# Two products of wo in split precision: M from hi and lo pieces in three one-pass matmuls a group

## The chip, the cores and the metric

The kernel runs on 1 core of a Trainium2 chip. The metric is device time in microseconds (us) for one execution, the median of several. TensorE (PE) does the matmuls, VectorE (DVE), ScalarE (ACT) and GpSimd (POOL) the element-wise work, and SyncE (SP) issues all DMA transfers. Each engine runs its own instructions in the order in which they were written, and waits on semaphores of the others.

## The reference

Two layers; each is a linear-attention block and an MLP with residuals, on 2048 rows of 448 floats (16 heads of 28, MLP width 1792).

```python
def _A_ref(x, wqkv, wo):
    qkv = (lambda x, *d: x.transpose(*d))((x @ wqkv).reshape(B, S, 3, H, Dh), 2, 0, 3, 1, 4)
    q, k, v = qkv[0], qkv[1], qkv[2]
    phi = lambda t: jnp.where(t > 0, t + 1, jnp.exp(t)) + 1e-6
    pq, pk = phi(q), phi(k)
    kv = jnp.einsum("bhsd,bhse->bhde", pk, v)
    z = jnp.einsum("bhsd->bhd", pk)
    num = jnp.einsum("bhqd,bhde->bhqe", pq, kv)
    den = jnp.einsum("bhqd,bhd->bhq", pq, z)[..., None] + 1e-6
    o = num / den
    return (lambda x, *d: x.transpose(*d))(o, 0, 2, 1, 3).reshape(B, S, D) @ wo
...
x = x + _A_ref(_layernorm(x, axis=-1), A_wqkv, A_wo)
x = x + _B_ref(_layernorm(x, axis=-1), B_w1, B_b1, B_w2, B_b2)
x = x + _A_ref(_layernorm(x, axis=-1), A_wqkv, A_wo)
x = x + _B_ref(_layernorm(x, axis=-1), B_w1, B_b1, B_w2, B_b2)
```

## The kernel before, in words

Float32 matmuls take several passes on TensorE. Nearly all products are therefore split: an operand x becomes hi (rounded to the one-pass type, by a copy on ACT) and lo = x - hi (on DVE or POOL), and hi*hi + hi*lo + lo*hi is summed in PSUM by three one-pass matmuls. Few products are left in plain float32, among them the one this case is about.

A layer has three parts.

**Phase 1** walks over 16 tiles of 128 rows (`phase1`, steps t = 0 to 15). Each step has a list of tokens (`STEP`, `STEPS`) that is carried out in that order: K projects a tile to k (`stage_k`), `kp`, `kh`, `kl` make phi(k) and its hi and lo (ek on ACT, L323 and L324; psk on DVE, L326; kh on ACT, L446; kl on DVE, L455) and add it to the running sum `za` (L462), `s` splits the normalized x (xnh on ACT, L428; xnl on POOL, L429), G adds x^T phi(k) of the tile before to four PSUM banks (`stage_g`, L508 to L512), Q projects to q (`stage_q`, psq), and in layer 0 `bg` splits a piece of an MLP weight behind that (hi w2h on ACT, L365; lo w2l on POOL, L366). In the last step the sum za becomes zh (ACT, L465) and zl (DVE, L468). After step 11 the piece of wqkv for v is loaded, and after step 13 `trans_load` issues two DMAs for `wo` (the tile wot, L643): groups 0 and 1 in the first, groups 2 and 3 in the second.

**The transition** (token list `ORDER`) turns these sums into one matrix M for the layer, 448 x 448 in four groups of 112 rows (four heads each). `z` multiplies zh and zl with ones (zp, L649) and makes zb (ACT, L651) and dc (DVE, L654, L655). `gt` copies G out of PSUM, `kv` multiplies it with wv into kvp (L669), `mask` keeps the blocks on the diagonal (kvm, L673). `m0` to `m3` each multiply a group of kvm with a group of wo (L679, PSUM mp), and `ms0` to `ms3` split the result into Mh (ACT, L691) and Ml (DVE, L692). Meanwhile the first four tiles of phi(q) are loaded, multiplied with zb (`qz`, pz on POOL, L722), divided by their denominators (`qs`: dn, L728 and L729, rd, L731, and pq, L733, all on DVE), transposed on PE (`tq`, L740) and split (`qq`: qh on ACT, L749, ql on DVE, L750); `Qp` gives phi(q) of a late tile (three ACT instructions, L496 to L498, and an addition on POOL, L499). `o0` to `o3` multiply with M (L760 to L762), and `la`, `lb` add the residual and normalize.

**The MLP** runs over four blocks of 512 rows (L829 to L849), with the attention output of the next block made behind it.

Buffers come from tagged pools: "H" has nine of 448 floats (tiles of x), "xn" and "F" two each of 512, "S" five of 1024. A new tile waits until the last user of an old one in its tag is done. In the last steps of layer 0 the "xn" buffers hold pieces of w2; "F" holds kl, zl and later the last Ml.

The order of the transition, cut to the part around M:

```python
    ORDER = (
        "Q ld1 z ld0 ld2 qz0 qz1 G gt qs1 Q Qp kv qs0 tq1 Q mask qz2 tq0 qs2 ld3 b "
        "m0 qq1 Qp m1 qz3 Qp ms0 qq0 m2 ms1 m3 ms2 tq2 ms3 qs3 o0 la0 qq2 o1 tq3 lb0 tu0 la1 qq3 "
```

Of the kernel before, what the change touches and what calls it, by code (L numbers as in the profile page):

```python
# [12 lines left out]
OP = mybir.AluOpType  # L13
# [9 lines left out]
def linear_attn_mlp_kernel(  # L23
# [43 lines left out]
    def t448(tag, bufs, name, dt=F32):  # L67
        bufs = NH if tag == "H" else bufs
        return work.tile([128, D], dt, name=name, tag=tag, bufs=bufs)
# [4 lines left out]
    def f(ap):  # L74
        return ap.bitcast(F32)
# [426 lines left out]
    def stage_g(l, t, acc):  # L502
# [16 lines left out]


    ORDER = (
# [3 lines left out]
    )  # L525
# [54 lines left out]
    def phase1(l, tr):  # L580
        za = consts.tile([128, D], F32, name="za", tag="za")
        acc = []
        load_to(l, 4 if l == 0 else NORM[l][1][-1])
        if l == 0:
            launch(za)
            load_to(l, NORM[l][2][-1])
        for t in range(l == 0, NT):
            norm = NORM[l][t] if t < len(NORM[l]) else ()
            for tok in STEPS.get((l, t), STEP).split():
                if tok[1:].isdigit() and tok[0] in "anv":  # L590
                    {"a": stage_a, "n": stage_n, "v": stage_t}[tok[0]](l, int(tok[1:]))
                elif tok == "q1":
                    stage_qphi(1)
                elif tok == "sp":
                    for key, h in list(stored):
                        block(key)
                        spread(key, h)
                elif tok == "ld" and t + 2 < len(NORM[l]):
                    load_to(l, NORM[l][t + 2][-1])
                elif tok == "a":  # L600
                    for u in norm:
                        stage_a(l, u)
                elif tok == "n":
                    for u in norm:
                        stage_n(l, u)
                elif tok == "tu":
                    for u in norm:
                        stage_t(l, u)
                elif tok == "T" and t + 1 < NT:
                    stage_b(l, t + 1, "acc" if t == 1 else "h")  # L610
                elif tok == "X" and t + 1 < NT and (l == 0 or t + 1 >= 4):
                    stage_x(l, t + 1)
                elif tok == "K":
                    stage_k(l, t)
                elif tok == "qp":
                    stage_qphi()
                elif tok == "kp":
                    stage_kphi(l, t)
                elif tok == "kh":
                    stage_kh(l, t)  # L620
                elif tok == "kl":
                    stage_kl(l, t, za)
                elif tok == "s":
                    stage_s(l, t)
                elif tok == "G" and t >= 1:
                    acc = acc or [bank("acc", 4, f"G{c}")[:, :D] for c in range(4)]
                    stage_g(l, t - 1, acc)
                elif tok == "bg" and l == 0:
                    background(BG[t], 1 if t >= 8 else 2)
                elif tok == "Q" and t < DEFER:  # L630
                    stage_q(l, t)
            if t == 11:
                tr.wv = stage_square(wqkv[:, 2 * D:])
            if t == 13:
                trans_load(l, tr)
        return za, acc


    def trans_load(l, tr):
        tr.wo = []  # L640
        for h in range(2):
            s = half("wot")[:G, :2 * D].rearrange("p (g n) -> p g n", g=2)
            sp.dma_start(s, wo[h * 2 * G:(h + 1) * 2 * G, :].rearrange("(g p) n -> p g n", p=G))  # L643
            tr.wo += [s[:, 0], s[:, 1]]

    def trans_z(tr, za):
        zp = bank("m", 2, "zp")[:, :D]
# [16 lines left out]
    def trans_kv(tr):  # L664
        tr.kvp = bank("m", 2, "kvp")[:G, :D]
        for g in range(NG):
            s = slice(g * G, (g + 1) * G)
            for c in range(4):
                pe.matmul(tr.kvp[:, s], tr.wv[c][:, s], tr.gt[c][:, s], start=(c == 0), stop=(c == 3))  # L669

    def trans_mask(tr):
        tr.kvm = t448("W6", 1, "kvm")[:G]
        dve.tensor_tensor(tr.kvm.rearrange("p (g d) -> p g d", g=NG),  # L673
                          tr.kvp.rearrange("p (g d) -> p g d", g=NG),
                          mask[:, None, :].to_broadcast([G, NG, G]), op=OP.mult)

    def trans_m(tr, g):
        mp = bank("acc", 4, "mp")[:G, :D]
        pe.matmul(mp, tr.kvm[:, g * G:(g + 1) * G], tr.wo[g], start=True, stop=True)  # L679
        tr.mp[g] = mp  # L680

    def trans_ms(tr, g):
# [263 lines left out]
    warm_up(2)  # L946

    for l in range(LAYERS):
        tr = SimpleNamespace(mp={})
        za, acc = phase1(l, tr)  # L950
        if l == 0:
            background(0)
        fill = list(range(DEFER, NT))

        def biases(j):
            if l == 0:
                sp.dma_start(b1s, b1.rearrange("(c p) -> p c", p=128))
                sp.dma_start(b2b, b2[None, :].to_broadcast([128, D]))

        def pre(j):  # L960
            for k in range(4):
                load_pq(l, 1, k)
            if l == 0:
                background(2)

        tok_ = SimpleNamespace(
            Q=lambda j: stage_q(l, fill.pop(0)), Qp=lambda j: fill_qphi(), Qv=lambda j: stage_qphi(j or 9),
            Qa=lambda j: stage_q(l, fill.pop(0), tag="acc"), G=lambda j: stage_g(l, NT - 1, acc),
            ld=lambda j: (load_pq(l, 0, j), load_x(l, j)), z=lambda j: trans_z(tr, zs[l]), gt=lambda j: trans_gt(tr, acc),
            kv=lambda j: trans_kv(tr), mask=lambda j: trans_mask(tr), m=lambda j: trans_m(tr, j),  # L970
            ms=lambda j: trans_ms(tr, j), qz=lambda j: q_z(l, 0, j, tr), qs=lambda j: q_scale(l, 0, j, tr),
            tq=lambda j: q_transpose(l, 0, j), qq=lambda j: q_split(l, 0, j), o=lambda j: o_mm(l, 0, j, tr),
            la=lambda j: o_ln(l, 0, j), lb=lambda j: o_n(l, 0, j), T=lambda j: m_transpose(l, 0, j),
            x=lambda j: m_split(l, 0, j), tu=lambda j: turn(xns.pop(("m", l, j)), ("m", l, 0), j),
            st=lambda j: store_sq(("m", l, 0), 0), sp=lambda j: spread(("m", l, 0), 0), pre=pre, b=biases)
        for tok in ORDER.split():
            name, j = tok.rstrip("0123456789"), int("0" + tok.lstrip("abcdefghijklmnopqrstuvwxyzQTG"))
            getattr(tok_, name)(j)
        assert not fill and not qo
        table(AF.Gelu_apprx_tanh)  # L980
        q_z(l, 1, 0, tr)
        mlp1(l, 0, 0)
        trans_chunks(tr)
        for b in range(NB):
            acc = [bank("acc", 4, f"y{j}")[:, :D] for j in range(4)]
            nxt = b + 1 < NB
            if not nxt and l + 1 < LAYERS:
                st_k = stage_square(wqkv[:, D:2 * D])
                st_q = stage_square(wqkv[:, :D])
                load_to(l + 1, PRE - 1)  # L990
            for i in range(NF):
                if i + 1 < NF:
                    mlp1(l, b, i + 1)
                elif nxt:
                    mlp1(l, b + 1, 0)
                if l == 0 and b == 0 and i:
                    background(1, 1)
                if i == NF - 2 and not nxt and l + 1 < LAYERS:
                    table(AF.Exp)
                if 9 <= i < 13:  # L1000
                    add_bias(l, b, i - 9)
                if nxt:
                    behind(l, b, i, tr)
                elif l + 1 < LAYERS:
                    if i == 2:
                        split_kq("k", st_k)
                    if i == 5:
                        split_kq("q", st_q)
                    if i in (3, 4, 6, 7, 8):
                        t = (3, 4, 6, 7, 8).index(i)  # L1010
                        stage_a(l + 1, t)
                        stage_n(l + 1, t)
                        stage_t(l + 1, t)
                        if t % 2:
                            stage_sp(l + 1, t)
                    if 9 <= i < 13:
                        stage_x(l + 1, i - 9)
                mlp2(l, b, i, acc)
# [28 lines left out]
```

## Time and profile before

| | us |
|---|---|
| median of 3 runs | 877.67 (877.45 to 877.82) |
| profiled execution, its own time | 878.36 |
| profiled execution, span from first to last instruction | 876.6 |
| PE busy in the span | 871.2 (99%) |
| DVE, ACT, POOL busy | 491.0, 344.2, 221.4 |

All times inside the span are counted from its first instruction. A row of the timeline gives the start, the duration, engine, line, operation, tiles (out<-in) and shape of an instruction or of a run of equal ones, and in brackets the idle time of the engine before it and what ended it. The transition of layer 0 lies at 104 to 139 us, that of layer 1 at 534 to 569 us. Instructions of an engine overlap a little, so that the distance between starts is shorter than a duration.

### The profile page before, as it was taken

The page shows a single profiled execution, that of the slowest core. Times are in us where ns is not written, and L with a number is a line of the kernel's source. Part 1 is how long each engine was busy: PE and PEld are TensorE (multiplying, and loading weights), DVE is VectorE, ACT ScalarE, POOL GpSimd, SP SyncE. Part 2 cuts the span into 40 slices and gives each one's busy share as a digit, 9 for nine tenths or more (in the row PEclk, how much of TensorE's full clock was granted, in tenths as well). Part 3 has the DMA queues.
Part 4 walks back from the last instruction along what each step waited for, and adds up shares of the span by engine and source line. Part 5 has one row for each costly group of instructions (what it writes and reads, how often), then busy time and mean ns, then how long its engine had stood idle before and what let it go on. Part 6 is the DMA issues. An engine that isn't in the chain of part 4 may idle for free.

```text
span 876.6 us, 11680 instructions
## 1 busy us (share of the span) xinstructions
PE 871.2 (99%) x4180; PEld 772.3 (88%) x4180; DVE 491.0 (56%) x957; ACT 344.2 (39%) x604; POOL 221.4 (25%) x250
## 2 busy tenths in 40 slices
PE   9999999999999999999999999999999999999998
PEld 8999988888888888888899998888888888888887
DVE  6878595658455443226467876864674473433112
ACT  5676635324223322333355665332233133223221
POOL 5566532335012102011222344120220140140000
PEclk9999999999999999999999999999999999999999
DMA  5475636624313402051145543352332413111001
GB/s 158 138 225 164 208 88 203 191 85 133 132 59 104 156 0 97 1 179 49 48 135 184 169 133 106 101 184 81 108 111 91 135 68 116 49 49 42 1 1 43
DMA packets 63482, 94.76 MB, mean 108 GB/s; under 512 B 8896, under 2 KB 58560, under 8 KB 63424
## 3 DMA queue, kind: packets, MB, share of 16 engines
q1 hardware_dynamic: 63424, 94.01, 33.4%
q8 instruction: 33, 0.54, 0.3%
q14 instruction: 25, 0.20, 0.1%
HBM read 56.17 MB, written 34.60 MB: 104 GB/s over the span
## 4 chain that ended last, share of the span: by engine, by line
PE 98%; DMA 1%; DVE 0%; issue 0%; POOL 0%; SPq 0%; POOLq 0%; DVEq 0%
PE y L849 10%; PE y L848 10%; PE y L847 10%; PE hp L830 9%; PE hp L829 9%; PE hp L831 9%; PE hp L832 3%; PE hp L833 3%; PE psk L313 2%; PE psq L312 2%; PE G L510 2%; PE psq L314 2%; PE G L508 2%; PE G L509 2%; PE psq L313 2%; PE psk L314 2%
## 5 line engine op out<-in xcount | busy, mean ns | idle before, releaser
L839 DVE TENSOR_TENSOR gl<-g,gh 128x512 fp32r<-128x512 f32 x112 | 82.6, 737 | 299.8 <-ACT gh L838 299.8
L835 ACT ACTIVATE g<-hp,b1s 128x512 f32<-128x512 f32 x112 | 77.1, 688 | 406.3 <-PE hp L833 403.4
L849 PE MATMUL y<-w2h,gl 128*128 128x448 f32 x448 | 163.7, 365 | 0.0
L848 PE MATMUL y<-w2l,gh 128*128 128x448 f32 x448 | 163.6, 365 | 0.0
L847 PE MATMUL y<-w2h,gh 128*128 128x448 f32 x448 | 163.6, 365 | 0.0
L830 PE MATMUL hp<-XH,w1l 128*128 128x512 f32 x336 | 131.5, 392 | 0.0
L829 PE MATMUL hp<-XH,w1h 128*128 128x512 f32 x336 | 131.2, 391 | 0.0
L831 PE MATMUL hp<-XL,w1h 128*128 128x512 f32 x336 | 131.2, 391 | 0.0
L209 POOL TENSOR_TENSOR brs<-bve,mhalf 128x1 f32<-128x1 f32 x64 | 39.6, 619 | 283.7 <-DVE bve L207 280.6
L847 PEld LDWEIGHTS y<-w2h,gh 128*128 128x128 f32 x448 | 84.1, 188 | 9.0
L848 PEld LDWEIGHTS y<-w2l,gh 128*128 128x128 f32 x448 | 84.1, 188 | 8.4
L849 PEld LDWEIGHTS y<-w2h,gl 128*128 128x128 f32 x448 | 84.2, 188 | 6.6
L831 PEld LDWEIGHTS hp<-XL,w1h 128*128 128x128 f32 x336 | 63.1, 188 | 14.2 <-issue 0.6
L830 PEld LDWEIGHTS hp<-XH,w1l 128*128 128x128 f32 x336 | 63.1, 188 | 11.2
L829 PEld LDWEIGHTS hp<-XH,w1h 128*128 128x128 f32 x336 | 63.1, 188 | 10.9
L838 ACT CAST gh<-g 128x512 fp32r<-128x512 f32 x112 | 69.7, 622 | 3.6
L722 POOL TENSOR_TENSOR pz<-pq,zb 128x448 f32<-128x448 f32 x32 | 36.6, 1146 | 84.4 <-DVE dn L728 69.6
L429 POOL TENSOR_TENSOR xnl<-x,xnh 128x384 fp32r<-128x384 f32 x32 | 35.0, 1093 | 72.4 <-ACT xnh L428 40.4
L302 DVE TENSOR_TENSOR XL<-sp,XH 128x512 fp32r<-128x512 f32 x50 | 44.2, 891 | 3.6 <-ACT XH L301 3.6
L833 PE MATMUL hp<-XL,w1x 128*128 128x512 f32 x112 | 43.6, 389 | 0.0
L832 PE MATMUL hp<-XH,w1x 128*128 128x512 f32 x112 | 43.6, 389 | 0.0
L791 POOL TENSOR_TENSOR x<-x,b2b 128x448 f32<-128x448 f32 x32 | 41.9, 1330 | 0.0
(152 smaller groups left out, 1567.1 us busy)
## 6 DMA issues: line engine op xcount, KB each, us to landing
x<-in_A_x_dram SPq DMA_DIRECT2D x32, 224.0 KB, 4.0
pq_d<-eq SPq DMA_DIRECT2D x32, 224.0 KB, 2.7
pq<-pq_d SPq DMA_DIRECT2D x32, 224.0 KB, 3.2
sq_m<-sq SPq DMA_DIRECT2D x14, 512.0 KB, 2.7
sp<-sq_m SPq DMA_DIRECT2D x56, 128.0 KB, 2.8
x<-x_d SPq DMA_DIRECT2D x32, 224.0 KB, 3.5
sq_a<-sq SPq DMA_DIRECT2D x12, 512.0 KB, 2.9
sp<-sq_a SPq DMA_DIRECT2D x48, 128.0 KB, 2.9
```

The source lines that it names most:

```text
L302: eng.tensor_tensor(lo.rearrange("p (c i n) -> p c i n", c=4, n=32), x, f(h), op=OP.subtract)
L829: pe.matmul(o, w1h[:, c, s], x.moving(x.hi, c), start=(c == 0), stop=False)
L830: pe.matmul(o, w1l[:, c, s], x.moving(x.hi, c), start=False, stop=False)
L831: pe.matmul(o, w1h[:, c, s], x.moving(x.lo, c), start=False, stop=False)
L832: pe.matmul(o, w1x[:, s], x.moving(x.hi, 3), start=False, stop=False)
L833: pe.matmul(o, w1x[:, s], x.moving(x.lo, 3), start=False, stop=True)
L835: act.activation(g, hp, AF.Gelu_apprx_tanh, bias=b1s[:, i:i + 1])
L838: act.copy(gh, g)
L839: dve.tensor_sub(gl, g, f(gh))
L847: pe.matmul(acc[j], gh[:, s], w2h[:, i], start=first, stop=False)
L848: pe.matmul(acc[j], gh[:, s], w2l[:, i], start=False, stop=False)
L849: pe.matmul(acc[j], gl[:, s], w2h[:, i], start=False, stop=last)
```

## The change

M is made from split operands. wo is split into woh (ACT copies, L653 of the changed kernel) and wol (DVE subtractions, L659): woh of groups 0 and 1 at the end of step 14, woh of groups 2 and 3 and wol of group 0 at the end of step 15, and wol of groups 1 to 3 at the new token `wol` behind `z`. The five buffers woh0 to woh3 and wol0 are of tag "H", wol1 and wol2 of "xn", wol3 of "F". The masked kvm is copied to kvh on ACT as part of `mask`, and kvl = kvm - kvh is made on DVE at the new token `mlo` behind `qs2`; both lie in a new "S" buffer. Each group of M is then three one-pass matmuls instead of one float32 matmul.

```diff
@@ ORDER
-        "Q ld1 z ld0 ld2 qz0 qz1 G gt qs1 Q Qp kv qs0 tq1 Q mask qz2 tq0 qs2 ld3 b "
+        "Q ld1 z wol ld0 ld2 qz0 qz1 G gt qs1 Q Qp kv qs0 tq1 Q mask qz2 tq0 qs2 mlo ld3 b "
@@ phase1, end of step t
             if t == 13:
                 trans_load(l, tr)
+            if t >= 14:
+                wo_hi(tr, (t * 2 - 28, t * 2 - 27))
+            if t == 15:
+                wo_lo(tr, (0,))
@@
+    def wo_hi(tr, gs):
+        for g in gs:
+            hi = t448("H", 8, "woh", F32R)[:G]
+            act.copy(hi, tr.wo[g])
+            tr.woh.append(hi)
+
+    def wo_lo(tr, gs):
+        for g in gs:
+            lo = (t448("H", 8, "wol", F32R) if g == 0 else t512("F" if g == 3 else "xn", 2, "wol", F32R)[:, :D])[:G]
+            dve.tensor_tensor(lo, tr.wo[g], f(tr.woh[g]), op=OP.subtract)
+            tr.wol.append(lo)
@@ trans_mask
+        s = work.tile([128, 1024], F32R, name="kvs", tag="S", bufs=5)[:G]
+        tr.kvh, tr.kvl = s[:, :D], s[:, 512:512 + D]
+        act.copy(tr.kvh, tr.kvm)
+
+    def trans_mlo(tr):
+        dve.tensor_tensor(tr.kvl, tr.kvm, f(tr.kvh), op=OP.subtract)
@@ trans_m
-        pe.matmul(mp, tr.kvm[:, g * G:(g + 1) * G], tr.wo[g], start=True, stop=True)
+        s = slice(g * G, (g + 1) * G)
+        pe.matmul(mp, tr.kvh[:, s], tr.woh[g], start=True, stop=False)
+        pe.matmul(mp, tr.kvh[:, s], tr.wol[g], start=False, stop=False)
+        pe.matmul(mp, tr.kvl[:, s], tr.woh[g], start=False, stop=True)
```

More of the change, by code (lines that the diff above doesn't have):

```diff
@@ L948, in linear_attn_mlp_kernel @@
     for l in range(LAYERS):
-        tr = SimpleNamespace(mp={})
+        tr = SimpleNamespace(mp={}, woh=[], wol=[])
         za, acc = phase1(l, tr)
@@ L969, in linear_attn_mlp_kernel @@
             ld=lambda j: (load_pq(l, 0, j), load_x(l, j)), z=lambda j: trans_z(tr, zs[l]), gt=lambda j: trans_gt(tr, acc),
-            kv=lambda j: trans_kv(tr), mask=lambda j: trans_mask(tr), m=lambda j: trans_m(tr, j),
+            kv=lambda j: trans_kv(tr), mask=lambda j: trans_mask(tr), mlo=lambda j: trans_mlo(tr), wol=lambda j: wo_lo(tr, (1, 2, 3)), m=lambda j: trans_m(tr, j),
             ms=lambda j: trans_ms(tr, j), qz=lambda j: q_z(l, 0, j, tr), qs=lambda j: q_scale(l, 0, j, tr),
```

## The prediction

> **What bounds the kernel now.** I read the engines' busy time first, then the chain that ended last, then the timeline of the transitions engine by engine.
>
> ```profile
> PE 871.2 (99%) x4180; PEld 772.3 (88%) x4180; DVE 491.0 (56%) x957; ACT 344.2 (39%) x604; POOL 221.4 (25%) x250
> PE 98%; DMA 1%; DVE 0%; issue 0%; POOL 0%; SPq 0%; POOLq 0%; DVEq 0%
> ```
>
> PE never rests: a PE instruction saved is time saved, and any wait that reaches PE is time lost. The other engines only have slack, and the question is how much of it lies where the new work goes.
>
> **M itself.** The timeline of PE in layer 0:
>
> ```profile
> 109.47 3.31 PE L669 MATMUL kvp<-gt,stg 128*112 128x112 f32 x32
> 112.61 0.60 PE L740 MATMUL tq<-ident,pq 128*112 128x128 f32 x4
> ...
> 115.72 3.17 PE L679 MATMUL mp<-wot,kvm 112*112 112x448 f32 x8
> 118.73 0.60 PE L740 MATMUL tq<-ident,pq 128*112 128x128 f32 x4
> 119.09 0.45 PE L760 MATMUL op<-Mh,qh 112*128 112x448 f32 x1
> 119.38 0.37 PE L761 MATMUL op<-Ml,qh 112*128 112x448 f32 x1
> ...
> 121.61 0.37 PE L760 MATMUL op<-Mh,qh 112*128 112x448 f32 x1
> ```
>
> The four float32 groups take 118.73 - 115.72 = 3.01 us. A one-pass matmul of the same width takes (121.61 - 119.38) / 11 = 0.203, and the first behind transposes 0.29. Twelve take 0.29 + 11 x 0.203 = 2.52. The change removes 0.49 a layer, 0.98 in all. That is all it can gain.
>
> **The copies of wo on ACT.** In layer 0 the SP queue, what the tile wot answers on its first DMA, and ACT, in this order:
>
> ```profile
> 96.97 1.50 SPq L643 DMA_DIRECT2D wot<-in_A_wo_dram  x1
> ```
> ```profile
> DMA to landing us min/median/max: 5.5/5.5/5.5
> ```
> ```profile
> 98.59 0.56 ACT L365 CAST w2h<-stg 128x448 fp32r<-128x448 f32 x1
> 99.05 0.57 ACT L428 CAST xnh<-x 128x448 fp32r<-128x448 f32 x1
> 100.19 0.54 ACT L323 ACTIVATE ek<-psk 128x448 f32<-128x448 f32 x1 [0.56 <-PE psk L317]
> ...
> 103.89 1.03 ACT L365 CAST w2h<-stg 128x448 fp32r<-128x448 f32 x2
> 105.21 0.63 ACT L651 ACTIVATE zb<-zp,zc 128x448 f32<-128x448 f32 x1 [0.29 <-PE zp L649]
> ```
>
> Groups 0 and 1 of wo land at 96.97 + 5.5 = 102.47. In the order of the changed program their two copies stand on ACT right behind the w2h of 98.59 and ahead of xnh, with a wait for that DMA. ACT keeps its order, so xnh, ek, kh and zh of tile 15, which want to start from 99.05 on, queue behind a transfer that is 3.4 us away. A copy in a row takes 0.47 (two in 1.03 with the last one's tail). The copies start near 102.53, xnh near 103.47, ek at 103.94 instead of 100.19: 3.75 late. PE beside DVE:
>
> ```profile
> 104.24 0.37 PE L317 MATMUL psq<-wq,XL 128*128 128x448 f32 x1
> ...
> 104.70 0.47 PE L649 MATMUL zp<-zl,ones 128*128 128x448 f32 x1
> ```
> ```profile
> 104.02 0.63 DVE L468 TENSOR_TENSOR zl<-za,zh 128x448 fp32r<-128x448 f32 x1 [0.16 <-ACT zh L465]
> ```
>
> zl ends at 104.65 and PE uses it at 104.70: this path has no slack. ek, psk, kh, za, zh, zl follow each other, so zp with zl moves to 108.45. PE has behind 104.24 nothing ahead of `z` in its order. **Stall in layer 0: 3.75.** From below it is the landing less the place of the copies, 102.47 - 99.06 = 3.4.
>
> In layer 1 the same pair is covered:
>
> ```profile
> 514.24 3.45 SPq L643 DMA_DIRECT2D wot<-in_A_wo_dram  x2
> ```
> ```profile
> DMA to landing us min/median/max: 5.6/6.0/6.5
> ```
> ```profile
> 527.94 0.56 ACT L428 CAST xnh<-x 128x448 fp32r<-128x448 f32 x1
> 530.01 0.55 ACT L323 ACTIVATE ek<-psk 128x448 f32<-128x448 f32 x1 [1.52 <-PE psk L317]
> ```
>
> Both have landed by 514.24 + 3.45 + 6.5 = 524.2, and two copies (0.94) fit in the 1.52 idle ahead of ek. Cost nothing. The copies of groups 2 and 3 lie behind zh. In layer 0 they put off the second w2h, and zb by about 0.6; in layer 1 there is no w2h and zb keeps its place.
>
> **wol on DVE, against POOL.** DVE and POOL in layer 1, where a denominator meets POOL's work:
>
> ```profile
> 538.05 0.62 DVE L728 TENSOR_REDUCE dn<-pz 128x16 f32<-128x448 f32 x1 [1.11 <-POOL pz L722]
> 538.70 0.17 DVE L729 TENSOR_TENSOR dn<-dn,dc 128x16 f32<-128x16 f32 x1
> ...
> 539.20 0.63 DVE L733 SCALAR_TENSOR_TENSOR pq<-pq,rd 128x448 f32<-128x448 f32 x1
> ...
> 540.38 0.92 DVE L729 TENSOR_TENSOR dn<-dn,dc 128x16 f32<-128x16 f32 x1
> ...
> 541.63 1.22 DVE L733 SCALAR_TENSOR_TENSOR pq<-pq,rd 128x448 f32<-128x448 f32 x1
> 542.77 0.61 DVE L673 TENSOR_TENSOR kvm<-kvp,mask 112x448 f32<-112x448 f32 x1
> ```
> ```profile
> 535.75 2.26 POOL L722 TENSOR_TENSOR pz<-pq,zb 128x448 f32<-128x448 f32 x2 [5.89 <-ACT zb L651]
> 540.15 1.13 POOL L499 TENSOR_TENSOR eq<-ep,eq 128x448 f32<-128x448 f32 x1 [2.14 <-ACT eq L498]
> 541.24 1.13 POOL L722 TENSOR_TENSOR pz<-pq,zb 128x448 f32<-128x448 f32 x1
> ```
>
> A DVE instruction with two inputs from SBUF does not run while such a POOL instruction runs: L729 takes 0.17 alone and 0.92 behind L499, ending where that ends (541.30, 541.28); L733 waits the same way for pz. The wol and kvl subtractions are of this kind. They cost 0.55 each when alone, and up to one POOL instruction (1.13) more, and hold POOL up in turn.
>
> The Trainium skill ("SBUF — State Buffer", Who interferes with whom) calls this an exclusive lock that the earlier issue gets for a whole instruction; by it a subtraction that comes first would wait for nothing. The trace shows the waiting side only.
>
> *Layer 1.* wol0 fits behind zl. dc ends as before, and pz runs until 535.75 + 2.26 = 538.01. wol1 waits for it, and the three end at 538.01 + 3 x 0.55 = 539.65, where dn started at 538.05: DVE is 1.5 late. L729 then meets L499 (until 541.3), rd and pq of tile 1 end at 542.25. The next pz waits for the buffer that the second dn (until 542.8) reads, so it runs 542.85 to 544.0 and blocks pq of tile 0 until 544.55. kvm moves from 542.77 to 544.5, its copy kvh ends at 545.7, and qs2 (dn, L729, rd, L733: 1.6) and kvl follow kvm on DVE: kvl ends at 547.3.
>
> PE around M in layer 1:
>
> ```profile
> 545.55 3.17 PE L679 MATMUL mp<-wot,kvm 112*112 112x448 f32 x8
> 548.56 0.60 PE L740 MATMUL tq<-ident,pq 128*112 128x128 f32 x4
> ```
>
> The second row lies 429.83 behind its twin in layer 0 (118.73), and I carry PE's, ACT's and DVE's rows of layer 0 over by that. M started at 545.55; now it starts at 545.75, when kvh is there, and its third matmul waits for kvl until 547.35. The other nine follow at 0.203, and M ends at 549.55 instead of 548.56 (0.17 of it a weight load not hidden).
>
> Then ACT, and DVE behind it, in layer 0:
>
> ```profile
> 113.25 0.59 ACT L749 CAST qh<-tq 112x512 fp32r<-112x512 f32 x1 [3.01 <-PE tq L740]
> ...
> 116.81 0.53 ACT L691 CAST Mh<-mp 112x448 fp32r<-112x448 f32 x1
> ```
> ```profile
> 118.52 1.68 DVE L692 TENSOR_TENSOR Ml<-mp,Mh 112x448 fp32r<-112x448 f32 x3
> ```
>
> kvh stands on ACT ahead of qh, so qh and the six Qp instructions behind it (3.56 with 0.44 of idle: 3.1 of work) wait for it. qh starts at 545.6, and Mh0 at 545.6 + 3.1 = 548.7 instead of 116.81 + 429.83 = 546.64, and Ml0, ql, Ml1 to Ml3 end at 552.15 instead of 118.52 + 1.68 + 429.83 = 550.03. `o0` is fed by these one at a time and hands over to `o1` at 552.7 instead of 551.44. **Layer 1: +1.3**, the 0.49 of M included.
>
> *Layer 0*, in old times (3.75 taken off). zb is late by 0.6, the two w2l on POOL (1.13 each) come ahead of pz, and wol0, dc's second instruction and wol1 to wol3 alternate with POOL's w2l, pz, pz and L499. wol3 ends at 112.6. The row this moves, and its cover:
>
> ```profile
> 109.05 0.62 DVE L728 TENSOR_REDUCE dn<-pz 128x16 f32<-128x448 f32 x1 [2.23 <-POOL pz L722]
> ```
>
> The 2.23 idle would hold three subtractions of 0.55 if nothing else moved. With the alternation dn starts at 112.55, 3.5 late; pq of tile 1 is ready at 114.3 where `tq1` wanted it at 112.61 (stall 1.7). The rest goes as in layer 1: kvm at 116.5, kvl until 119.3, M over at 121.35 instead of 118.73, `o1` at 124.7 instead of 121.61. **Layer 0 behind the stall: +3.2**, with 0.1 for ql of tile 2.
>
> Behind `o3` DVE has idle again, and the loads of x and of wq are not issued later than PE moves. New buffers: "S" gets one more tile between wv and Mh, released long before; the "H" tiles take buffers of x tiles 7 to 11. Both cost nothing; I see no gain or loss but in the two transitions.
>
> **Sum.** 3.75 + 3.2 + 1.3 = 8.25 on the profiled execution's 878.36 (span 876.6): 886.6. That execution lies 0.69 over the median of the runs, 877.67, so the forecast is 885.9. Bounds of the lock: if wol and kvl cost 0.55 each and never wait, dn is 0.3 late in both layers and the kvh, qh, Mh order on ACT alone is left, about +0.4 and +0.1 with M's gain in: 3.75 + 0.5 = 4.25, 881.9. If kvl also waits for a POOL instruction in each layer, 2 x 1.13 more: 888.2.
>
> **Rivals.**
> - *The stall without the lock* (881.9). For: which engine gets in first is a race, and 2.23 and 1.11 of idle stand ahead of dn. Against: L729 and L733 show the blocking, and POOL has instructions waiting. 0.20.
> - *PE goes cold in its 3.3 us of idle.* At the start of the kernel PE is slow:
>
> ```profile
> 1.50 4.64 PE L162 MATMUL warm<-ones 128*128 128x128 f32 x20 [1.50 <-DVE ones L157]
> ```
>
>   0.232 each, against 3.14 / 32 = 0.098 for kvp's 112 columns, or 0.112 for 128. If PE falls back to that half rate for 4.64 us, it loses 2.3: 888.2. 0.10. The Trainium skill ("TensorE: Matmul & The Clock Gate", Part 1) has the clock halved after a window of about 3.4 us without work, from 104.6 to 107.8 here nearly one. No gap of that size stands in this trace behind the start, and the granted clock reads 1.00 even there.
> - *Faster.* The mechanism is the copies of wo finding their data there. It takes a landing before 99.06, so an issue before 93.6; SP issues wot at 96.97, behind transfers that the change does not touch. Then only the lock is left, and if that does not bite either, M's 0.98 gives 878.36 - 0.98 - 0.69 = 876.7. 0.03, of which 0.01 for the lock eating the gain.
> - *Beyond 889*, more waits than I followed: 0.05.
>
> The change does what it says: PE's order has the twelve matmuls in place of the four, so that is no rival.
>
> **How the numbers follow.** The forecast, stall and lock, has 0.62. The range 881.5 to 888.8 holds it, the stall without the lock, kvl waiting on top, and the cold PE; it leaves out some 0.1 to 0.15. Two thousandths are 1.8 us, about what can be told from no change: faster 0.02, same 0.01, slower 0.97.
>
> **What would show it.** Right: ACT idle for over 3 us ahead of L653 in layer 0, ended by the DMA of wot; PE idle about as long ahead of zp; L659 rows longer than 0.62; a PE wait ahead of the third matmul of M (L704); twelve matmuls in 2.5 plus that wait. Wrong: woh copies in layer 0 that start before 100, wol rows of 0.6 and dn within 0.5 of its place, or matmul spacing of 0.4 behind zp.

## The result, and the profile after

The changed kernel takes **884.50 us** (median of 6 runs, 884.17 to 885.74) against 877.75 (6 runs, 877.43 to 878.22) of the kernel before on the same chip: ratio 1.0078, interval 1.0067 to 1.0089, slower by 6.75. The forecast was 885.9, its range 881.5 to 888.8. The profiled execution took 884.17, with a span of 882.4.

The page of the changed kernel, engines and then the chain that ended last:

```profile
PE 872.4 (99%) x4188; PEld 773.4 (88%) x4188; DVE 499.5 (57%) x967; ACT 347.8 (39%) x614; POOL 223.2 (25%) x250
PE 87%; DVE 6%; issue 3%; ACT 2%; POOL 1%; DMA 1%; SPq 0%; DVEq 0%; ACTq 0%; POOLq 0%
```

PE is busy for as long as before (872.4 against 871.2) although M is shorter; among other things, some matmuls ran at a lower clock (below). The chain now leaves PE for 13% of the span, where it was 2%; half of that is DVE.

A warning ahead of all comparisons of starts: the two profiled executions do not keep the same pace ahead of the transition. The first matmul of phase 1 starts at 7.46 in the kernel before and at 6.85 in the changed one (the other runs of this case have 6.75 to 7.46), and from 50 to 95 us matmuls are spaced 0.207 in the one and 0.202 in the other. So all rows of the changed kernel are 1.15 early when the transition of layer 0 begins (the last psq matmul ahead of `z`, L317, starts at 103.09 instead of 104.24). I therefore count from that matmul in each layer, and call what is left a **shift**.

**Layer 0, the stall.** ACT's timeline (start, duration, engine, line, operation, tiles; in brackets the idle time ahead and what ended it):

```profile
97.49 0.56 ACT L365 CAST w2h<-stg 128x448 fp32r<-128x448 f32 x1
100.84 1.03 ACT L653 CAST woh<-wot 112x448 fp32r<-112x448 f32 x2 [2.79 <-DMA wot<-in_A_wo_dram]
101.78 0.56 ACT L428 CAST xnh<-x 128x448 fp32r<-128x448 f32 x1
...
105.47 0.56 ACT L465 CAST zh<-za 128x448 fp32r<-128x448 f32 x1 [0.74 <-DVE za L462]
...
107.81 0.62 ACT L667 ACTIVATE zb<-zp,zc 128x448 f32<-128x448 f32 x1
```

The copies of wo (woh) wait 2.79 for their DMA, with xnh and the rest of step 15 behind them. PE's timeline, and then the row of the stretch 107 to 111 us in the windows (busy time of PE, PEld, DVE, ACT and POOL, then PE's granted clock as a share of full speed, DMA share, GB/s):

```profile
103.09 0.37 PE L317 MATMUL psq<-wq,XL 128*128 128x448 f32 x1
106.09 0.48 PE L665 MATMUL zp<-zh,ones 128*128 128x448 f32 x1 [2.63 <-ACT zh L465]
106.75 0.47 PE L665 MATMUL zp<-zl,ones 128*128 128x448 f32 x1 [0.18 <-DVE zl L468]
...
107.46 0.51 PE L510 MATMUL G<-kh,xnl 128*128 128x448 f32 x1
107.78 0.57 PE L508 MATMUL G<-kh,xnh 128*128 128x448 f32 x1
...
110.39 0.57 PE L512 MATMUL G<-kl,xnh 128*128 128x448 f32 x1
```
```profile
107.00:111.00 4.00, 4.00 (x13) 3.56 (x13) 3.71 (x5) 1.85 (x4) 3.75 (x4) 0.57 0.00 0
```

zp with zl starts 3.20 late (shift). From 107.46 to 110.76 the matmuls of G come every 0.37 in place of 0.20, and the mean granted clock of these 4 us is 0.57. I call this state of PE cold.

**Layer 0, DVE, ACT and PE up to M:**

```profile
106.61 1.60 DVE L659 TENSOR_TENSOR wol<-wot,woh 112x448 fp32r<-112x448 f32 x1
109.23 3.59 DVE L659 TENSOR_TENSOR wol<-wot,woh 112x448 fp32r<-112x448 f32 x3
112.75 0.61 DVE L753 TENSOR_REDUCE dn<-pz 128x16 f32<-128x448 f32 x1
...
117.00 0.61 DVE L689 TENSOR_TENSOR kvm<-kvp,mask 112x448 f32<-112x448 f32 x1
...
119.22 0.62 DVE L697 TENSOR_TENSOR kvs<-kvm,kvs 112x448 fp32r<-112x448 f32 x1
...
121.84 0.62 DVE L717 TENSOR_TENSOR Ml<-mp,Mh 112x448 fp32r<-112x448 f32 x1 [1.41 <-ACT Mh L716]
```
```profile
117.65 0.57 ACT L694 CAST kvs<-kvm 112x448 fp32r<-112x448 f32 x1 [3.85 <-DVE kvm L689]
118.12 0.58 ACT L774 CAST qh<-tq 112x512 fp32r<-112x512 f32 x1
...
121.24 0.56 ACT L716 CAST Mh<-mp 112x448 fp32r<-112x448 f32 x1
```
```profile
119.24 0.45 PE L702 MATMUL mp<-woh,kvs 112*112 112x448 f32 x1
...
119.89 0.46 PE L704 MATMUL mp<-woh,kvs 112*112 112x448 f32 x1
...
122.02 0.60 PE L765 MATMUL tq<-ident,pq 128*112 128x128 f32 x4
```

The three wol take 3.59, where three of 0.55 make 1.65; dn starts at once behind them, and kvm starts at 117.00: shift +4.83. M takes 122.02 - 119.24 = 2.78. But look at ACT: kvh, qh and two Qp run without a gap from 117.65 to 121.24, and only then comes the first Mh, 0.6 later the first Ml. The third matmul of group 0, at 119.89, was not what they waited for.

**Layer 1**, DVE and the third matmul of M:

```profile
541.20 2.64 DVE L659 TENSOR_TENSOR wol<-wot,woh 112x448 fp32r<-112x448 f32 x3
543.76 0.60 DVE L753 TENSOR_REDUCE dn<-pz 128x16 f32<-128x448 f32 x1
...
548.31 0.61 DVE L689 TENSOR_TENSOR kvm<-kvp,mask 112x448 f32<-112x448 f32 x1
```
```profile
551.20 0.46 PE L704 MATMUL mp<-woh,kvs 112*112 112x448 f32 x1 [0.73 <-DVE kvs L697]
```

**Where a layer's delay comes out.** The first row below is DVE's, the last XL that the MLP needs; the second PE's, the matmul that uses it. First the changed kernel, then the kernel before:

```profile
143.25 0.68 DVE L258 TENSOR_TENSOR XL<-tp,XH 128x512 fp32r<-128x512 f32 x1
144.07 0.47 PE L856 MATMUL hp<-XL,w1h 128*128 128x512 f32 x1 [0.45 <-DVE XL L258]
```
```profile
117.38 0.62 DVE L692 TENSOR_TENSOR Ml<-mp,Mh 112x448 fp32r<-112x448 f32 x1 [1.16 <-ACT Mh L691]
...
138.89 0.68 DVE L258 TENSOR_TENSOR XL<-tp,XH 128x512 fp32r<-128x512 f32 x1
139.72 0.47 PE L831 MATMUL hp<-XL,w1h 128*128 128x512 f32 x1
```

After, PE waits there for DVE. Before, the same matmul shows no wait to speak of: XL ends at 139.57, and PE uses it at 139.72. From the first Ml to this matmul it is 139.72 - 117.38 = 22.34 before and 144.07 - 121.84 = 22.23 after; in layer 1 it is 22.34 and 22.21. **So the end of a transition is set by when the first Ml is done, and from there by a row of work that VectorE leads; in the kernel before, TensorE arrived there at the same moment.** The row is not quite unbroken: in both kernels VectorE waits in it three times, 0.73 for GpSimd's `brs` and 1.37 and 0.29 for ScalarE, 2.39 in all, and what it waits for stands behind VectorE's own results.

That splits the loss of a layer into three: the shift of kvm, the change of the way from kvm to the first Ml, and a remainder of about -0.1. Layer 0: +4.83, from 4.06 to 4.84 (+0.78), -0.11: +5.51. Layer 1: +1.20, from 4.44 to 4.83 (+0.39), -0.13: +1.47. Together 6.98, beside 6.75 between the medians.

### The profile page after: what moved, and what is told of

Read it like the earlier page. It is cut to its first block, busy times and chain, and to the rows that moved or that the text cites. A ratio compares the mean times of both kernels' runs of the same rounds, so it can differ in the third digit from the quotient of the medians.

```text
span 882.4 us, 11721 instructions
## 1 busy us (share of the span) xinstructions
PE 872.4 (99%) x4188; PEld 773.4 (88%) x4188; DVE 499.5 (57%) x967; ACT 347.8 (39%) x614; POOL 223.2 (25%) x250
## 4 chain that ended last, share of the span: by engine, by line
PE 87%; DVE 6%; issue 3%; ACT 2%; POOL 1%; DMA 1%; SPq 0%; DVEq 0%; ACTq 0%; POOLq 0%
PE y L874 10%; PE y L872 10%; PE y L873 10%; PE hp L856 9%; PE hp L855 9%; PE hp L854 9%; PE hp L858 3%; PE hp L857 3%; PE psk L313 2%; PE psk L314 2%; PE psk L312 2%; PE op L797 2%; PE op L796 2%; PE op L798 2%; PE G L508 2%
```

## The experiments

Every kernel ran beside the kernel before on the same chip. The table gives for each the shifts in layer 0 and layer 1 (worked out from starts in its trace), the sum of the two shifts of the MLP's matmul, and the median with its difference. The sum of the shifts gives the measured difference within 0.75 us throughout. Six medians (wo_early, warm, no_lo, early_no_lo, mlo_first, qp_last) lie 0.2 to 0.4 outside the range of the view that they support; fit, pool_lo and the three chain kernels lie outside all ranges that were expected.

| kernel | kvm | first Ml | MLP's matmul | sum | median (difference) |
|---|---|---|---|---|---|
| the change | +4.83, +1.20 | +5.61, +1.60 | +5.51, +1.47 | 6.98 | 884.50 (+6.75) |
| wo_early | +2.00, +1.20 | +2.77, +1.60 | +2.66, +1.50 | 4.16 | 881.68 (+3.87) |
| warm | +4.60, +1.21 | +5.38, +1.60 | +5.30, +2.06 | 7.36 | 885.16 (+7.35) |
| no_lo | +3.67, +0.01 | +4.44, +0.40 | +4.34, +0.30 | 4.64 | 882.59 (+4.78) |
| early_no_lo | +1.13, +0.01 | +1.90, +0.41 | +1.79, +0.30 | 2.09 | 879.38 (+1.57) |
| wol_psum | +1.13, +0.01 | +1.91, +0.41 | +1.80, +0.30 | 2.10 | 879.60 (+1.64) |
| mlo_first | +2.00, +1.20 | +2.77, +1.60 | +2.67, +1.49 | 4.16 | 881.88 (+3.92) |
| qp_last | +1.97, +1.20 | +1.99, +0.85 | +2.14, +0.98 | 3.12 | 880.63 (+2.67) |
| fit | +1.77, +1.98 | +1.78, +1.62 | +1.91, +1.75 | 3.66 | 881.39 (+3.43) |
| pool_lo | +1.79, +0.01 | +4.11, +1.96 | +4.22, +1.83 | 6.05 | 884.33 (+6.56) |
| chain_before | -0.51, -0.13 | -0.57, -0.58 | +4.76, +5.17 | 9.93 | 887.51 (+9.63) |
| chain | +0.36, -0.14 | +0.76, -0.68 | +6.61, +6.62 | 13.23 | 891.00 (+13.12) |
| chain_wol | +0.72, -0.06 | -0.09, -0.72 | +6.38, +5.60 | 11.98 | 890.59 (+12.71) |

### The stall alone: wo_early

```diff
-            if t == 13:
+            if t == 12:
                 trans_load(l, tr)
```

> The changed kernel with the two DMAs of wo issued after step 12 instead of 13, so ahead of the w2 piece on which the SP queue waits. Theory (ACT waits for the landing of wo in layer 0, PE waits behind it and then runs cold): the copies of wo find their data, PE's idle ahead of zp shrinks from 3.2 us to under 0.6, the eleven matmuls of G behind it go back from 0.37 to 0.20 us each; about 3.5 to 4.5 us less than the changed kernel's 884.5, some of it given back because DVE's lock waits are then no longer covered: 880.5 to 881.5. Rival (the extra instructions on ACT and DVE are the cost, wherever the data land): under 1 us less, 883.5 to 884.5.

881.68 (881.32 to 881.98), ratio 1.0044 [1.0031, 1.0056]: 2.8 less than the change. ACT's copies and DVE's subtractions:

```profile
97.95 1.03 ACT L653 CAST woh<-wot 112x448 fp32r<-112x448 f32 x2
```
```profile
106.33 3.65 DVE L659 TENSOR_TENSOR wol<-wot,woh 112x448 fp32r<-112x448 f32 x3
109.90 0.61 DVE L753 TENSOR_REDUCE dn<-pz 128x16 f32<-128x448 f32 x1
```

The copies wait for nothing, PE is not idle ahead of `z` and not cold; the shift of kvm in layer 0 falls from 4.83 to 2.00. That is the stall's share, 2.83. What is left, 3.87, is not the stall.

### The cold PE alone: warm

14 matmuls whose result is not used stand ahead of `z` in layer 0, so that PE has work while it waits.

```diff
+        if l == 0:
+            w = bank("h", 2, "w")
+            for _ in range(14):
+                pe.matmul(w[:, :D], ones, wkq["q", 3], start=True, stop=True)
         zp = bank("m", 2, "zp")[:, :D]
```

> The changed kernel with 14 one-pass matmuls into a spare PSUM bank ahead of z in layer 0 (their result is not used), so that PE works through the wait for wo. Theory that the slow matmuls of G behind the wait (0.37 us each instead of 0.20, 1.5 us in all) come from PE's idle time: they go back to 0.20. On the time two views differ. The slow clock is paid in full: 1.3 to 1.5 us less, 883.1. DVE's chain (wol, dn, kvm, kvl) sets M's third matmul anyhow, and PE only arrives there earlier and waits longer: 884.2 to 884.8, no change.

885.16 (884.83 to 885.64), ratio 1.0084 [1.0070, 1.0098]: nothing gained. The clock was granted in full (the same window as above), and PE then waits ahead of M instead:

```profile
107.00:111.00 4.00, 4.00 (x21) 3.70 (x21) 3.71 (x5) 3.31 (x8) 3.75 (x4) 1.00 0.00 0
```
```profile
119.94 0.46 PE L708 MATMUL mp<-woh,kvs 112*112 112x448 f32 x1 [0.95 <-DVE kvs L701]
```

The eleven matmuls of G, nine of them slow, cost 1.47 on PE (110.39 + 0.37 - 107.06 against 11 x 0.203), but kvm comes only 0.23 earlier when they run at full speed. DVE sets the time there. The executions of the changed kernel agree: the one with a mean granted clock of 1.000 took 884.45, the four at 0.998 took 884.17 to 885.08 (a sixth, at 0.996, took 885.74). In this run layer 1 takes 0.55 more behind the first Ml, for a reason that is not the edit's: ScalarE waits there for a DMA to land, where in the changed kernel it does not wait.

```profile
572.76 1.14 ACT L301 CAST XH<-sp 128x512 fp32r<-128x512 f32 x2 [0.47 <-DMA sp<-sq_m]
```

### The subtractions of wol: no_lo and early_no_lo

The second product takes woh in place of wol, and the subtractions are left out, so that M lacks the low part of wo. early_no_lo loads wo earlier as well.

```diff
-            dve.tensor_tensor(lo, tr.wo[g], f(tr.woh[g]), op=OP.subtract)
-            tr.wol.append(lo)
+            tr.wol.append(tr.woh[g])
```

> The changed kernel without the four wol subtractions on DVE; the second product of each group takes woh again, so lo of wo is left out of M. Theory (wol meets POOL's instructions and makes dn, kvm and kvl late): kvm in layer 1 is 1.3 us earlier, the wait ahead of M's third matmul in layer 1 (0.9 us) goes, o0 starts earlier; 1.0 us less in layer 1 and 0.3 to 0.6 in layer 0, where PE's slow stretch covers most: 882.9 to 883.2. Rival (kvh ahead of qh on ACT is what makes M's split late): under 0.4 us less.

882.59 (882.51 to 883.40), ratio 1.0057 [1.0043, 1.0070]: 1.9 less than the change.

> Both: wo issued after step 12, and no wol (lo of wo left out of M). Theory: landing and lock are the whole loss but for the kvh, kvl chain; 877.7 to 879, within 1.3 us of the kernel before. Rival: the rest of the loss lies elsewhere (later in the kernel), then over 880.

879.38 (879.21 to 881.08), ratio 1.0019 [1.0011, 1.0028]: 5.1 less than the change, where the single edits add up to 4.7. So stall and subtractions nearly add up, and 1.57 of the 6.75 belongs to neither. This kernel also answers what became of M's gain. Layer 1, PE, DVE, and PE again, this kernel first (its lines are 2 lower behind L659) and then the kernel before:

```profile
534.74 0.36 PE L317 MATMUL psq<-wq,XL 128*128 128x448 f32 x1
...
549.06 0.44 PE L783 MATMUL op<-Mh,qh 112*128 112x448 f32 x1
...
570.52 0.47 PE L854 MATMUL hp<-XL,w1h 128*128 128x512 f32 x1 [0.43 <-DVE XL L258]
```
```profile
548.29 0.62 DVE L715 TENSOR_TENSOR Ml<-mp,Mh 112x448 fp32r<-112x448 f32 x1 [1.41 <-ACT Mh L714]
```
```profile
534.07 0.36 PE L317 MATMUL psq<-wq,XL 128*128 128x448 f32 x1
...
548.92 0.45 PE L760 MATMUL op<-Mh,qh 112*128 112x448 f32 x1
...
569.55 0.47 PE L831 MATMUL hp<-XL,w1h 128*128 128x512 f32 x1
```
```profile
547.21 0.62 DVE L692 TENSOR_TENSOR Ml<-mp,Mh 112x448 fp32r<-112x448 f32 x1 [1.54 <-ACT Mh L691]
```

Counted from psq, `o0` starts 14.32 behind in place of 14.85: M's shorter row is there, 0.53 on PE. But the first Ml comes at 13.55 in place of 13.14, 0.41 later, and the MLP's matmul at 35.78 in place of 35.48. It follows Ml, not `o0`. The gain on TensorE is spent waiting for XL (0.43 in the brackets): in this order of the tokens M's saving gives nothing.

### Lock or VectorE's own time: wol_psum

The three subtractions read z's PSUM tile in place of wo, so that one input comes from SBUF. Their results are then not the low parts of wo; their count and place stay, and all else is as in wo_early.

```diff
-            dve.tensor_tensor(lo, tr.wo[g], f(tr.woh[g]), op=OP.subtract)
+            dve.tensor_tensor(lo, tr.zp[:G] if g else tr.wo[g], f(tr.woh[g]), op=OP.subtract)
```

> Baseline as above, 881.68. The three subtractions of wol for groups 1 to 3 read z's PSUM tile in place of wo, so each has one operand from SBUF in place of two; their count, size and place stay. The low parts of wo are then wrong numbers. If the three subtractions are long because they take turns with GpSimd whenever both inputs come from SBUF, the group of three takes about 1.7 to 2.0 us in place of 3.65, dn is 1.3 to 2 us earlier in layer 0 and about 1 us in layer 1, and the time is 879.5 to 880.3. If it is VectorE's own time for three more operations that matters, or GpSimd's loss elsewhere, the time stays at 881.4 to 881.9.

879.60 (879.21 to 880.34), ratio 1.0021 [1.0012, 1.0030]: 2.1 less than wo_early, and the same as with no subtractions at all. The durations of the six (ns: least, median, most),

```profile
L659 DVE TENSOR_TENSOR wol<-zp,woh x6: 608/613/620, 106.4 to 538.6; 112x448 fp32r<-112x448 f32 x6
```

and GpSimd's multiplications in the same stretch of layer 0:

```profile
106.33 2.26 POOL L747 TENSOR_TENSOR pz<-pq,zb 128x448 f32<-128x448 f32 x2
```

All six take 0.61 to 0.62; of the same six in wo_early three do, and three take 1.57 to 1.62. GpSimd is not held up either (2.26, and 2.65 in wo_early). Three more operations on VectorE cost nothing that can be seen in this place; the turns with GpSimd cost all of it. The rival is out.

### Third matmul or ScalarE: mlo_first and qp_last

mlo_first moves `mlo` right behind `mask` (the first line below), and qp_last in addition the third Qp behind M (the second). Both are built on wo_early.

```diff
-        "... Q mask qz2 tq0 qs2 mlo ld3 b "
-        "m0 qq1 Qp m1 qz3 Qp ms0 qq0 m2 ms1 m3 ms2 tq2 ms3 qs3 ..."
+        "... Q mask mlo qz2 tq0 qs2 ld3 b "
+        "m0 qq1 Qp m1 qz3 ms0 qq0 m2 ms1 m3 ms2 tq2 ms3 Qp qs3 ..."
```

> Baseline is the changed kernel with wo loaded one step earlier (881.68, ratio 1.0044). Here also the low part of the mask's tile, mlo, stands right behind mask in the hand-written order, ahead of qz2 and qs2. Only the order of VectorE's work changes, and the work is complete. If the time that is left is the delay of VectorE's chain mask, kvm, mlo, kvl, on which the third matmul of M waits 0.96 us in layer 0, that wait shrinks in both layers by the one or two operations moved past it: 879.7 to 880.2. If ScalarE's chain (kvh, qh, Qp, then Mh0) sets when o0 can start, M's wait only moves behind M: 881.2 to 881.5.

881.88 (881.50 to 881.97), ratio 1.0043 [1.0031, 1.0056]: no change against 881.68. PEld's waits in the transition of layer 0 (what was waited for, us in total, times, longest):

```profile
PEld op L785 <- ACT qh L774: 1.0, 1, 1.0
```

The wait ahead of the third matmul fell from 1.4 to 0.4 and came back in full ahead of `o0`. The way from kvm to the first Ml stayed at 4.83.

> As the kernel with mlo behind mask, and the third Qp, a copy on ScalarE that stands between the second and third group of M in the order, is moved behind the last copy of M (ms3). The work is complete. If the copies of M's high parts are late because ScalarE does Qp ahead of them, o0 starts earlier by about one such copy in each layer, and together with the earlier mlo the third matmul's wait and the wait for Mh both go: 879.5 to 880.2. If ScalarE's order is not what holds o0, nothing changes against the kernel with mlo behind mask alone (within 0.3 us).

880.63 (880.15 to 881.28), ratio 1.0031 [1.0020, 1.0043]: 1.25 less than mlo_first. The way from kvm to Ml falls to 4.07, while 0.26 and 0.24 are given back behind it, where the moved Qp now stands (22.49 and 22.47 in place of 22.23). So ScalarE's row of kvh, qh and Qp ahead of Mh sets this way. In the kernel before, no copy of kvm stood at the head of that row.

### A schedule for the change: fit

Low parts of all four groups behind qs0, copies of wo at four places, pz of tiles 0 and 1 on DVE, on top of qp_last.

```diff
-        "Q ld1 z wol ld0 ld2 qz0 qz1 G gt qs1 Q Qp kv qs0 tq1 Q mask ..."
+        "Q ld1 z ld0 ld2 G gt qz1 qs1 Q Qp kv qz0 qs0 wol tq1 Q mask ..."
```

> The work is complete; this is the changed kernel with a schedule made for it: wo loaded one step earlier; its four high parts copied at the ends of steps 14 and 15 and between the copies of step 15 of ScalarE; all four subtractions behind qs0, ahead of tq1, where they meet GpSimd's row of multiplications no more; two of the multiplications that GpSimd does on the first block (pz of tiles 0 and 1) on VectorE; mlo behind mask; the third Qp behind ms3. If the waits in the transition are all that the change pays, they go and the 0.49 us that M saves in each layer shows: 876.8 to 877.8. If the four subtractions ahead of tq1 hold VectorE as much as they did ahead of dn, kvl stays late and the time is 878.5 to 880.5.

881.39 (880.75 to 881.76), ratio 1.0037 [1.0023, 1.0051]: 0.8 more than qp_last, and above both expectations. dn is now early (1.65 in layer 0), but the subtractions hold kvm back where they stand now. In layer 1 they meet GpSimd again:

```profile
542.98 3.16 DVE L663 TENSOR_TENSOR wol<-wot,woh 112x448 fp32r<-112x448 f32 x4
```

### The low parts on GpSimd: pool_lo

On top of qp_last, wol of groups 1 to 3 is made by POOL, and woh of groups 2 and 3 behind zb.

```diff
-        "Q ld1 z wol ld0 ld2 qz0 qz1 G gt ... mask mlo qz2 tq0 ..."
+        "Q ld1 z wh ld0 ld2 qz0 qz1 wol1 G gt ... mask mlo qz2 wol2 wol3 tq0 ..."
-            dve.tensor_tensor(lo, tr.wo[g], f(tr.woh[g]), op=OP.subtract)
+            (pool if g else dve).tensor_tensor(lo, tr.wo[g], f(tr.woh[g]), op=OP.subtract)
```

> The changed kernel with wo loaded one step earlier, mlo behind mask and the third Qp behind M (that kernel: 880.63), and two more edits: the low parts of groups 1 to 3 are made by GpSimd, the first behind its first two multiplications pz, the others behind the third; and the copies woh of groups 2 and 3 stand behind zb on ScalarE, ahead of the copies of G. The work is complete. If the time that is left is the work that the change adds to VectorE ahead of kvm (wol of groups 1 to 3) and zb's delay in layer 0, kvm comes back to within 0.6 us of its place behind psq in the kernel before in both layers, and the time is 877.6 to 878.8. If GpSimd's subtractions hold VectorE's own through the shared port as much as VectorE's held GpSimd's, pq and kvl become longer by what wol leaves, and the time stays at 879.4 to 880.6.

884.33 (883.07 to 884.60), ratio 1.0073 [1.0059, 1.0086]: 3.7 more than qp_last, a miss on the far side of both expectations. Layer 1, POOL and DVE:

```profile
545.89 2.65 POOL L659 TENSOR_TENSOR wol<-wot,woh 112x448 fp32r<-112x448 f32 x2
```
```profile
547.59 1.44 DVE L697 TENSOR_TENSOR kvs<-kvm,kvs 112x448 fp32r<-112x448 f32 x1 [0.64 <-ACT kvs L694]
...
549.59 1.06 DVE L754 TENSOR_TENSOR dn<-dn,dc 128x16 f32<-128x16 f32 x1
```

In layer 1 kvm is back (shift +0.01), as the first theory said; in layer 0 it is not (+1.79, the addition to dn there takes 1.54). And kvl takes 1.44 in place of 0.62, beside the second subtraction on GpSimd, and the way from kvm to Ml becomes 6.39. So a subtraction on GpSimd holds VectorE up as well. The 1.06 of the addition to dn, in place of 0.17, is not a subtraction's doing: they are over at 545.89 + 2.65 = 548.54, and the addition ends with GpSimd's next instruction, the addition of Qp, which waited for ScalarE:

```profile
549.46 1.15 POOL L499 TENSOR_TENSOR eq<-ep,eq 128x448 f32<-128x448 f32 x1 [0.92 <-ACT eq L498]
```

VectorE, late by kvl, ran into it; in layer 0 the 1.54 covers the end of the first subtraction and the whole of L499.

### An order for the chain: chain, chain_wol, chain_before

kvm ahead of the multiplication of tile 0, `tq0` behind the second group of M, Qp behind M, and `qs2` behind ms2. chain and chain_wol load wo one step earlier; chain has `wol` of groups 2 and 3 behind `mlo`, chain_wol leaves all three ahead of dn. chain_before is the kernel before in this order.

```diff
-        "... qs1 Q Qp kv qs0 tq1 Q mask mlo qz2 tq0 qs2 ld3 b "
-        "m0 qq1 Qp m1 qz3 ms0 qq0 m2 ms1 m3 ms2 tq2 ms3 Qp qs3 o0 la0 qq2 o1 ..."
+        "... qs1 Q Qp kv qd0 mask qs0 mlo tq1 Q wp qz2 m0 qq1 m1 tq0 ld3 b "
+        "ms0 qz3 qq0 m2 ms1 m3 ms2 qs2 tq2 ms3 Qp qs3 o0 la0 qq2 Qp o1 ..."
```

> Theory after the runs so far: from the first Ml to the MLP's first wait the way is one chain on VectorE of 22.2 us in every kernel, so the end is set by when the first Ml is done, and the change made that later in two ways: kvm starts later (the stall and wol), and kvm to Ml takes 4.83 us in place of 4.06 and 4.44. M's shorter row on TensorE then gives nothing. This kernel has the whole change, wo loaded one step earlier, and an order made for that chain: only wol of group 1 ahead of dn, groups 2 and 3 behind mlo; kvm ahead of the multiplication by rd of tile 0; tq0 behind the second group of M; the third and second Qp behind M. The work is complete. If the theory holds, the first Ml is at least 0.4 us earlier behind psq than in the kernel before, TensorE becomes what ends last, and the 0.49 us a layer that M saves shows: 876.7 to 877.4. If the low parts behind mlo only move VectorE's delay behind kvm, the first Ml is late as before: 878.3 to 879.5.

> The same order, but all three subtractions of wol stand ahead of dn as in the changed kernel. The work is complete. By the theory kvm and the first Ml are late by what these three take beyond VectorE's wait for pz, some 1.4 us in layer 1 and up to 2 in layer 0, less what the earlier place of kvm gives back: 878.0 to 879.5. If the place of wol does not matter, the time is that of the kernel with wol split within 0.4 us.

> The kernel before, with M in its four-pass form, in the same order (kvm ahead of tile 0's multiplication, tq0 behind the second group of M, Qp behind M). The work is complete. In the kernel before TensorE waits only 0.07 us at the MLP's first wait and some tenths in the whole stretch, so TensorE ends there with VectorE: if that holds, an earlier chain on VectorE brings nothing: 877.3 to 877.9. If VectorE alone sets the end, the first Ml comes 0.6 to 0.9 us earlier a layer and the time is 876.2 to 876.8; then the order is worth that much in either form of M and the gain of the other kernel is not the change's.

891.00 (889.27 to 892.11), 890.59 (889.82 to 890.91) and 887.51 (886.67 to 888.00), ratios 1.0149, 1.0147 and 1.0110: all far off. In chain_before the first Ml came 0.57 and 0.58 earlier, about as meant, yet it is 27.7 and 28.1 from there to the MLP in place of 22.3. DVE and PE of chain_before, layer 0:

```profile
119.90 0.62 DVE L738 SCALAR_TENSOR_TENSOR pq<-pq,rd 128x448 f32<-128x448 f32 x1
```
```profile
120.63 0.62 PE L745 MATMUL tq<-ident,pq 128*112 128x128 f32 x4 [2.69 <-issue]
```

My own edit did that: `qs2` behind ms2 puts pq of tile 2 behind Ml, and the transposition tq2, which stands ahead of `o0` on PE, waits for it. Behind that wait PE is cold here too, and this time VectorE waits for it; the stretch 120 to 124 us, with the granted clock of 0.77:

```profile
120.00:124.00 4.00, 3.37 (x15) 3.12 (x16) 2.64 (x6) 0.00 (x0) 1.53 (x1) 0.77 0.18 61
```

Nine matmuls of `o0` from 122.10 on take 3.30 in place of 9 x 0.203 = 1.83. So 2.69 of waiting and 1.47 of slow clock make up most of the 5.33 that this layer loses behind the first Ml. The 22.2 us are no constant of the chip, only of an order behind Ml that the other kernels share. These three runs do not tell whether M's gain can be had with an earlier Ml; that stays open. No version here beats the kernel before.

## Why the prediction came out right, step by step

**M's saving.** Right in size: 2.78 with 0.15 of waiting in layer 0, and 0.53 on PE in layer 1 of early_no_lo, for 0.49. Wrong in worth. "A PE instruction saved is time saved" is the step that failed: it was read from a PE share of 99% over the whole span, and in the stretch between M and the MLP VectorE's row ends within 0.15 us of TensorE's. The 0.49 a layer that the sum took as gained was not on the path. With it failed "Behind `o3` DVE has idle again": that idle is 2.39 of waits inside the row that sets the end. So the prediction read each layer's delay at `o1` on PE; it had Mh 2.06 late in layer 1 (548.7 - 546.64) and let 1.3 of that through. In the run Mh is 1.57 late and 1.47 comes through.

**The stall.** Right in kind; 3.20 on PE in place of 3.75. The landing was the size that was off: the DMA was issued at 95.87 and the copies started 4.97 later, not 5.5. ACT's wait, 2.79, is a little under the 3 that the prediction named as a sign. The stall's share of the total, by wo_early, is 2.83.

**The cold PE.** Given a chance of 0.10 and a price of 2.3. It happened, in the profiled execution, and cost at most 0.23 (warm): DVE and POOL were the later ones anyway. The prediction's own list has "matmul spacing of 0.4 behind zp" as a sign of being wrong; 0.37 was seen, and it changed nothing. An event and its price are two questions: in chain_before, where VectorE waited for PE, the same slow stretch cost 1.47. The Trainium skill ("TensorE: Matmul & The Clock Gate", Part 1) has the half clock after an idle window of about 3.4 us and calls that window free-running. Here 2.63 of idle, a single matmul and 0.18 more were enough in this execution, and 2.24 were not in the profiled one of no_lo, whose clock read 1.00 from 107 to 111. Neither number can be read as a threshold, for two other executions of no_lo have a mean clock of 0.997. In chain_before a single gap of 2.69 was enough, less than that window.

**The lock.** Right, and now shown by wol_psum rather than argued. In layer 1 it moves kvm by 1.20, where 1.73 was forecast; in layer 0 by 0.87 (from 1.13 in wol_psum to 2.00 in wo_early). The rest of layer 0's shift, 1.13, is there without any wol, so it is not the lock on these; in early_no_lo the first dn is 0.61 late (shift), and the pq behind it takes 1.43 in place of 0.62, running into GpSimd's L499. zb starts 0.86 late there, 0.31 of it from ahead of `z` and the rest behind the copies of wo, which fits the prediction's 0.6; in pool_lo, where these copies stand behind zb, zb is 0.32 late. But no run takes those copies away alone. The forecast for layer 0 behind the stall was +3.2 and +5.51 - 2.83 = 2.7 came.

**kvh, qh, Qp, Mh on ACT.** Right: kvh to Mh is 121.24 - 117.65 = 3.59, forecast 3.6 (kvh ending at 545.7 and so starting near 545.1, Mh at 548.7), and qp_last takes part of it away. The wait of M's third matmul, which the prediction put in the same sum, was real and worth nothing (mlo_first).

**Sum.** 8.25 was forecast and 6.98 came (stall 0.9 less, layer 0 behind it 0.5 less, layer 1 0.2 more). M's 0.98, counted as gained, did not come, and the other parts were together 2.25 too large. That the sum is off by only 1.27 is in part luck: one error hid some of the other.

## What to carry to other kernels

Before you price a saving on the busiest engine, follow that engine to the next place where it meets another one, and look how late the other is there: here 0.49 us a layer came out as nothing, because VectorE's row ended at the same moment. A subtraction that splits an operand is cheap in a gap only if no GpSimd work runs in it; with one input in PSUM it took 0.61 us here, with both in SBUF 0.61 or some 1.6. And moving such work to the other of the two engines moved the wait here, it did not remove it.

## What the runs showed of the hardware

The turns with GpSimd go both ways: three subtractions on VectorE beside two multiplications on GpSimd take 3.65 and 2.65 (wo_early) in place of 1.68 and 2.26 (wol_psum), and a subtraction on GpSimd makes one of 0.62 on VectorE last 1.44 (pool_lo). The Trainium skill ("SBUF — State Buffer", Who interferes with whom) has the engine that issues first hold the port for a whole instruction, and the other block. The rows agree. In this row of several operations on each side they alternate: in wo_early GpSimd's two end at 107.46 and 108.96, and VectorE's at 107.94, 109.44 and 109.98. That is no fixed turn, though: in layer 0 of pool_lo an addition on VectorE that starts at 109.75 waits out a subtraction (until 110.16) and the GpSimd instruction right behind it (until 111.25). An operation with one PSUM input took no part (0.608 to 0.620 beside the same GpSimd work).
